# Causal half-width scores with exchanged key halves, and a different split of the output writes, in a decayed linear attention followed by a soft mixture of experts

## The chip, the core and the metric

One core of one Trainium2 chip (8 cores on two dies) runs the program in one launch. The metric is device microseconds of one execution. Times of the kernel before are the median of 3 runs; the profile is of one further execution.

## What is computed

Four batches, 8 heads, 768 positions, 64 channels. Attention without softmax decays by a factor lam per head and position and is computed in blocks with a carried state; its output, as 3072 rows of 512, goes through a soft mixture of 8 experts with 4 slots each.

```python
intra = einsum('bhic,bhjc->bhij', qb, kb) * Dmask      # Dmask[i, j] = lam**(i-j) if i >= j else 0
intra = einsum('bhij,bhjd->bhid', intra, vb)
inter = einsum('bhid,bhde->bhie', qb * lam_pow, kv_state)
out[block] = intra + inter
kv_state = lam**block * kv_state + einsum('bhsd,bhse->bhde', kb * rev_pow, vb)
...
logits = x @ phi                                       # x: 3072 x 512, phi: 512 x 32 slots
slot_input = softmax(logits, axis=0).T @ x
h = maximum(slot_input[e] @ w1[e], 0); slot_out[e] = h @ w2[e]      # 8 experts, 512 -> 1024 -> 512
return softmax(logits, axis=1) @ slot_out
```

Inputs come to 55.1 MB (16.8 MB for w1 and as much for w2 among them), the output to 6.29 MB, all in fp32.

## The kernel before, in words

**Order.** Every engine runs its instructions in the order in which the code issues them (class InOrder). All large loads and all output writes are issued by SyncE (SP) into one hardware queue; SP waits there for a free buffer, or for an earlier DMA.

**Attention (loop over t, lines 485 to 560).** 24 chunks of 128 positions, 6 per batch. For chunk t the loop issues loads for chunk t+2 (q and k turned to channels on the partitions, v, and k once more in natural layout for some chunks; 256 KB each, 12 buffers "ld") and, by the numbers PACE and AHEAD, about three 1 MB tiles of w1 per four chunks (17 buffers "slab"). Then:
- `scores(t)` (lines 223 to 238): for 4 head pairs hp, 2 key halves j and 2 heads hh one matmul with 64 keys as columns of the array and 128 queries moving. The head picks the upper or lower 64 rows of the array, the key half the left or right 64 columns, so four matmuls work in four quarters of the array at a time. Each fp32 matmul shows as two MATMULs.
- `masks(t)`: VectorE multiplies the scores by the decay mask, which is zero for keys behind the query, into `at`.
- `recall(t)`: queries times carried state. `turn_k`: k turned on TensorE for chunks whose natural k is not loaded. `natural(t-1)`: the last output turned to rows.
- `attend(t)` (lines 301 to 318): v times `at`, added to the recalled part; ScalarE copies the result `xt` out of PSUM.
- `state(t)`: decayed keys times v (16 MATMULs of 64 columns), VectorE adds, GpSimd decays. `decay_q`, `decay_k` on GpSimd prepare queries and keys of the next chunk. `kpow`, the decay of keys, is a view of the mask's last column.
- every fourth chunk `logits`, `weights`, `slots`: a running softmax over rows and the slots' inputs.

**Experts (from line 566).** After the last chunk 24 tiles of w2 of 256 KB ("w2t") go into freed buffers of the attention, and ten of 1 MB ("w2p") into slabs, one of them already in chunk 22. `first(0)`, `first(1)` multiply by w1 for four experts each; `shares` (line 700), in the middle of `first(0)`, turns the row softmax into `parts`, a rounded part and its remainder. `CR` (line 711) is an exact copy of the first 256 rows' share. `stack` (line 724) spreads the parts over partitions, in 16 casts of 32 partitions each per 1024 rows. `second(part, ...)` (line 676) multiplies by w2: 16 quads (four expert quarters at a time), part 0 for output columns 0 to 255 and part 1 for 256 to 511; quads 0 to 7 of a part use the first four experts, 8 to 15 the others, and each four need the next two 1 MB tiles.

**Outputs.** `take` copies a finished half of the slots' outputs out of PSUM (ScalarE one half, then VectorE the other); `spread` repeats it over partitions and splits it in two parts; `put(t, half)` makes 256 output rows times 256 columns with two matmuls, copies them on ScalarE or VectorE in turn, and issues the write. `fill` places such puts between the quads of part 1: PUTS says before which quad, 0 standing for a `spread`, n for n puts. Rows below 2*SPLIT*128 are written as two halves of 256 KB, the rest as whole rows of 512 KB.

```python
PUTS = ((2, (0, 1)), (6, (2,)), (8, (2,)), (10, (2,)))
SPLIT = 7
```

Of the kernel before, what the change touches and what calls it, by code (L numbers as in the profile page):

```python
# [14 lines left out]
P = 128  # L15
# [5 lines left out]
SL = 32  # L21
# [9 lines left out]

PUTS = ((2, (0, 1)), (6, (2,)), (8, (2,)), (10, (2,)))
SPLIT = 7
PACE = 76
# [3 lines left out]
def loaded(t):  # L38

    return t % NB in (2, 3) or t % (2 * NB) == 4  # L40


# [16 lines left out]
def decay_attn_soft_moe(  # L59
# [28 lines left out]
    phi_sb = const.tile([P, HP, SL], F32, name="phi_sb")  # L88
    phi_in = const.tile([P, HP, SL], F32, name="phi_in")

# [25 lines left out]
    def load_one(pool_, tag, bufs):  # L116
# [43 lines left out]
    def place_phi():  # L160
        for a in range(2):
            for hh in range(2):
                pool.tensor_copy(
                    out=phi_sb[64 * a:64 * a + 64, 2 * hh:2 * hh + 2],
                    in_=phi_in[64 * hh:64 * hh + 64].rearrange("c (g a) s -> c a g s", a=2)[:, a],
                )
# [15 lines left out]
    own4 = const.tile([P, 4], F32, name="own4")  # L182

    mask = work.tile([P, 2, HP, P], F32, tag="mask", name="mask")
    for hh in range(2):
        for hp in range(HP):
            x = hh * HP + hp
            dve.tensor_tensor_scan(
                out=mask[:, hh, hp, :],
                data0=lam_sb[:, x:x + 1].broadcast_to([P, P]),  # L190
                data1=ident,
                initial=0.0,
                op0=ALU.mult,
                op1=ALU.add,
            )
# [13 lines left out]
    lamc = qpow[:, :, P - 1:P]  # L209
    kpow = mask.rearrange("p a b i -> p (a b) i")[:, :, P - 1:P]  # L210
    CN = const.tile([P, T, SL], F32, name="CN")
    acc = const.tile([P, D], F32, name="acc")
    lsum = const.tile([P, 1], F32, name="lsum")
    e = const.tile([P, P], F32, name="e")
    d = const.tile([P, P], F32, name="d")
    L = const.tile([P, P], F32, name="L")

# [5 lines left out]
    def scores(t):  # L223
        q_, k_ = IN[t, 0], IN[t, 1]
        banks = [bank(x) for x in (("gl", "dp") if t == 0 else ("sc0", "sc1"))]

        for hp in range(HP):
            for j in range(2):
                for hh in range(2):
                    r = slice(64 * hh, 64 * hh + 64)  # L230
                    pe.matmul(
                        out=banks[hh][64 * j:64 * j + 64, hp * P:(hp + 1) * P],
                        lhsT=k_[r, hp * P + 64 * j:hp * P + 64 * j + 64],
                        rhs=q_[r, hp * P:(hp + 1) * P],
                        start=True,
                        stop=True,
                    )
        SC[t] = banks
# [45 lines left out]
    def recall(t):  # L284
        XB[t] = [bank("xa"), bank("xb")]
        if t % NB > 0:

            qs, st = QS.pop(t), ST["st"]
            for hp in range(HP):
                for hh in range(2):  # L290
# [8 lines left out]
                    )  # L299

    def attend(t):
        n = t % NB
        v_ = IN[t, 2].rearrange("p (h c) -> p h c", h=H)
        at = AT.pop(t)
        xt = keep.tile([P, HP, P], F32, tag="xt", name="xt")
        for hh in range(2):
            for hp in range(HP):
                pe.matmul(
                    out=place(t, hh, hp),
                    lhsT=v_[:, HP * hh + hp, :],  # L310
                    rhs=at[hh][:, hp, :],
                    start=(n == 0 and hp < 2),
                    stop=True,
                    skip_group_check=True,
                )
            copy = dve.tensor_copy if t == T - 1 and hh else act.copy
            copy(out=xt[:, 2 * hh:2 * hh + 2], in_=XB[t][hh][:, 0:2 * P].rearrange("p (a b) -> p a b", a=2))
        XT[t] = xt

    def state(t):  # L320
# [134 lines left out]

    blk = const.tile([P, 4, SL], F32, name="blk")
# [3 lines left out]
    const.tile([P, 8], F32, name="fill")  # L460
    sent = 0
    ld1 = (loads, "ld", NLOAD)
    sm = iter(())
    for t in range(T):
# [8 lines left out]
        if t == 0:  # L473
            sp.dma_start(out=phi_in, in_=phi)

# [111 lines left out]
    slots(G - 1)  # L587
    tr = bank("tr")
    for hp in range(HP):
        pe.transpose(tr[:, hp * P:(hp + 1) * P], XT[T - 1][:, hp, :], ident)  # L590
# [3 lines left out]
    act.copy(out=xl[:, 0:HD], in_=tr[:, 0:HD])  # L594
    dl = bank("dp")
    pe.transpose(dl[:, 0:P], el, ident)
    dn = small.tile([P, SL], F32, tag="dn", name="dn", bufs=1)
    dve.tensor_copy(out=dn, in_=dl[:, 0:SL])
    dve.tensor_copy(out=xl[:, HD:D], in_=tr[:, HD:D])

# [96 lines left out]
    load_one(keep, "x", 5)  # L697
    parts, CR = [], []

    def shares():  # L700
# [9 lines left out]
        act.copy(out=parts[0].bitcast(F32R), in_=parts[1])  # L710
        CR.append(half_slab("CR")[:, 0:2 * P].rearrange("p (t c) -> p t c", t=2))
        for n in range(16):
            b, c = divmod(n, 4)
            r = slice(SL * b, SL * b + SL)
            copy = (act.copy, pool.tensor_copy, dve.tensor_copy)[n % 3]
            copy(out=CR[0][SL * c:SL * c + SL, :, r], in_=parts[1][r, 0:2, :])

# [17 lines left out]

    stack((act.copy, pool.tensor_copy, dve.tensor_copy))
    stack((act.copy, pool.tensor_copy, dve.tensor_copy))
    first(1)
    stack((pool.tensor_copy,))
# [21 lines left out]
    def take(half, bank_):  # L761

        x = so[:, half * HD:(half + 1) * HD]
        act.copy(out=x[:, 0:P], in_=bank_[:, 0:P])
        dve.tensor_copy(out=x[:, P:HD], in_=bank_[:, P:HD])

    ow = {}

    def put(t, half):
# [4 lines left out]
        for i in range(2):  # L774
            c_ = CT[t // 8][:, t % 8:t % 8 + 2] if t else CR[0]
            pe.matmul(
                out=pf[:, i * HD:(i + 1) * HD],
                lhsT=c_.rearrange("k t p -> k (t p)").rearrange("k (p i) -> k i p", i=2)[:, i],
                rhs=s4[half] if t else so[:, half * HD:(half + 1) * HD],
                start=True,  # L780
# [12 lines left out]

    pairs = [(t, 0) for t in range(0, 2 * SPLIT, 2)] + [(0, 1)]
    pairs += [(t, 0) for t in range(2 * SPLIT, T, 2)]
    pairs += [(t, 1) for t in (*range(2 * SPLIT, T, 2), *range(2, 2 * SPLIT, 2))]
    pairs.reverse()
# [77 lines left out]
```

## Time and profile before

| | |
|---|---|
| median of 3 runs (lowest to highest) | 167.37 us (166.79 to 169.35) |
| the profiled execution's own time | 167.14 us |
| span of its program on the core | 165.3 us |
| mean granted TensorE clock | 0.976 |
| busy share PE, VectorE, GpSimd, ScalarE | 90%, 55%, 43%, 35% |
| the 16 DMA engines' share on SP's queue | 96.6% |

The profile is read by stage, since shares are means over stages with different limits: attention to about 109 us, w1 to 128 us, w2 to 147.5 us, then outputs alone. PE is TensorE's matmuls, PEld its weight loads, DVE VectorE, ACT ScalarE, POOL GpSimd, SP SyncE. A DMA's landing is its issue in SP's timeline plus the time to landing that the view of DMA issues gives.

### The profile page before, as it was taken

The page shows a single profiled execution, that of the slowest core. Times are in us where ns is not written, and L with a number is a line of the kernel's source. Part 1 is how long each engine was busy: PE and PEld are TensorE (multiplying, and loading weights), DVE is VectorE, ACT ScalarE, POOL GpSimd, SP SyncE. Part 2 cuts the span into 40 slices and gives each one's busy share as a digit, 9 for nine tenths or more (in the row PEclk, how much of TensorE's full clock was granted, in tenths as well). Part 3 has the DMA queues.
Part 4 walks back from the last instruction along what each step waited for, and adds up shares of the span by engine and source line. Part 5 has one row for each costly group of instructions (what it writes and reads, how often), then busy time and mean ns, then how long its engine had stood idle before and what let it go on. Part 6 is the DMA issues. An engine that isn't in the chain of part 4 may idle for free.

```text
span 165.3 us, 6275 instructions
## 1 busy us (share of the span) xinstructions
PE 149.1 (90%) x2651; PEld 109.0 (66%) x2651; DVE 90.3 (55%) x208; ACT 58.5 (35%) x147; POOL 71.8 (43%) x108
## 2 busy tenths in 40 slices
PE   6999999999989999999999999998999989989400
PEld 6778878677868878788868896863323455648300
DVE  2964445447744574568655775564388821328600
ACT  3134412443443444231635152242055902226400
POOL 2786790277447227766119665300022894000000
PEclk9999999999999999999999999999999999999955
DMA  5999999999999999999999999999999999982897
GB/s 165 357 418 392 312 363 414 410 423 401 412 416 402 417 409 408 410 350 344 402 415 401 415 391 394 404 390 367 375 336 396 418 416 423 396 302 76 362 402 251
DMA packets 25131, 61.82 MB, mean 374 GB/s; under 512 B 2576, under 2 KB 6288, under 8 KB 23056
## 3 DMA queue, kind: packets, MB, share of 16 engines
q1 hardware_dynamic: 24960, 61.42, 96.6%
q8 instruction: 21, 0.34, 0.7%
q14 instruction: 6, 0.05, 0.1%
q10 hardware_dynamic: 144, 0.01, 0.1%
HBM read 55.12 MB, written 6.29 MB: 371 GB/s over the span
## 4 chain that ended last, share of the span: by engine, by line
PE 66%; DVE 9%; DMA 5%; ACT 5%; POOL 4%; issue 3%; DVEq 0%; POOLq 0%; ACTq 0%
PE xa L53 17%; PE sc L53 14%; PE kv L53 10%; PE xb L53 8%; PE gl L53 8%; PE tr L53 7%; DMA w2t<-w_x 3%; DVE o L53 3%; ACT ct L53 2%; DVE mask L53 2%; DMA lam_sb<-lam_x 2%; POOL kd L53 2%; PE dp L53 2%; POOL qs L53 1%; DVE hz L53 1%
## 5 line engine op out<-in xcount | busy, mean ns | idle before, releaser
L53 DVE TENSOR_TENSOR at<-sc,mask 128x512 f32<-128x512 f32 x46 | 29.6, 685 | 15.4 <-PE sc L53 14.6
L53 ACT COPY x<-tr 128x512 f32<-128x512 f32 (+1 forms) x24 | 13.9, 578 | 37.7 <-PE tr L53 37.7
L53 POOL TENSOR_TENSOR qs<-ld,qpow 128x512 f32<-128x512 f32 x20 | 25.5, 1275 | 2.1 <-POOL kd L53 2.1
L53 PE MATMUL sc<-ld 64*64 64x128 f32 x736 | 26.0, 276 | 0.1
L53 PEld LDWEIGHTS sc<-ld 64*64 64x64 f32 x736 | 20.3, 133 | 6.2 <-issue 3.4
L53 POOL TENSOR_TENSOR dec<-st,qpow 128x256 f32<-128x256 f32 x16 | 9.9, 621 | 25.6 <-DVE st L53 25.5
L53 POOL TENSOR_TENSOR kd<-kn,mask 128x512 f32<-128x512 f32 x10 | 10.6, 1058 | 12.8 <-ACT kn L53 12.4
L53 PE MATMUL xa<-at,ld 128*64 128x128 f32 x192 | 15.8, 284 | 0.0
L53 DVE TENSOR_TENSOR st<-dec,kv 128x256 f32<-128x256 f32 x16 | 6.7, 422 | 16.5 <-PE kv L53 15.1
L53 PE MATMUL tr<-ident,xt 128*128 128x128 f32 x96 | 15.4, 283 | 0.0
L53 PE MATMUL xb<-at,ld 128*64 128x128 f32 x192 | 14.6, 273 | 0.1
L53 PE MATMUL xa<-qs,st 64*64 64x128 f32 x160 | 14.0, 274 | 0.7 <-POOL qs L53 0.3
L53 PE MATMUL xb<-qs,st 64*64 64x128 f32 x160 | 13.1, 274 | 0.6 <-issue 0.6
L53 PE MATMUL kv<-ld,kd 128*64 128x64 f32 x320 | 12.9, 223 | 0.1
L53 PEld LDWEIGHTS tr<-ident,xt 128*128 128x128 f32 x96 | 10.4, 141 | 3.8 <-issue 3.8
L53 POOL CAST ct<-part 32x256 fp32r<-32x256 f32 x26 | 10.3, 395 | 5.0 <-DVE part L53 3.9
L53 PEld LDWEIGHTS xa<-at,ld 128*64 128x64 f32 x192 | 10.0, 136 | 3.7 <-issue 1.6
L53 PEld LDWEIGHTS kv<-ld,kd 128*64 128x64 f32 x320 | 11.9, 138 | 0.8 <-issue 0.5
L53 PEld LDWEIGHTS xa<-qs,st 64*64 64x64 f32 x160 | 9.9, 133 | 3.0 <-issue 1.9
L53 PEld LDWEIGHTS xb<-at,ld 128*64 128x64 f32 x192 | 11.0, 137 | 0.3 <-issue 0.2
L53 POOL TENSOR_TENSOR kd<-ld,mask 128x512 f32<-128x512 f32 x10 | 10.6, 1059 | 0.0
L53 PEld LDWEIGHTS xb<-qs,st 64*64 64x64 f32 x160 | 9.4, 133 | 0.2 <-ACT xt L53 0.2
(148 smaller groups left out, 233.8 us busy)
## 6 DMA issues: line engine op xcount, KB each, us to landing
slab<-w_x SPq DMA_DIRECT2D x16, 1024.0 KB, 8.4
w2p<-w_x SPq DMA_DIRECT2D x10, 1024.0 KB, 10.6
ld<-qT SPq DMA_DIRECT2D x24, 256.0 KB, 6.8
ld<-kT SPq DMA_DIRECT2D x24, 256.0 KB, 6.5
ld<-vN SPq DMA_DIRECT2D x24, 256.0 KB, 7.5
w2t<-w_x SPq DMA_DIRECT2D x24, 256.0 KB, 5.4
y<-o SPq DMA_DIRECT2D x14, 256.0 KB, 4.0
ld<-kN SPq DMA_DIRECT2D x10, 256.0 KB, 7.2
```

What stands on the lines that cost most here:

```text
L53: return self._tc.keep_in_program_order(f(*args, **kwargs))
```

## The change

**Scores.** From chunk 2 on, matmuls of the second key half take only the 64 queries that can see them. For head pairs 2 and 3 (`plain` is false) the two key halves change places in the array and in PSUM; their mask is built from an identity with exchanged halves (`d`), `vs` holds v of these heads with exchanged halves, copied by ScalarE in two copies of 64 partitions after each `attend`, and `kpow` becomes a tile of its own, put together by three VectorE copies. Score banks are the same two tiles from chunk 1 on.

**Experts and outputs.** `CR` goes; all outputs use the parts. The second of the three `stack` calls moves behind `first(1)`. The last four units of w2 come as two DMAs of 1 MB by row half i instead of by expert pair. `take` is one ScalarE copy. Part 1 has one spread before quad 8 and nine first-half puts before quad 12, with no puts elsewhere; behind it one first half, then second halves, with the last three row groups as whole rows.

```diff
-PUTS = ((2, (0, 1)), (6, (2,)), (8, (2,)), (10, (2,)))
-SPLIT = 7
+PUTS = ((8, (0,)), (12, (9,)))
+SPLIT = 9
...
+def plain(hp):
+    return hp < HP // 2
...
+    def load_four():
+        Q, x, _ = units[-1]
+        units.clear()
+        for i in range(2):
+            t_ = slabs.tile([P, 4, 512], F32, tag="slab", name="w2p")
+            src = w2[4 * Q:4 * Q + 4, x:x + 2].rearrange("e x p d -> e (x p d)")
+            sp.dma_start(out=t_, in_=src.rearrange("e (p i d) -> i p e d", p=P, i=2)[i])
...
+    for j in range(2):
+        dve.tensor_copy(out=d[:, 64 * j:64 * j + 64], in_=ident[:, 64 - 64 * j:128 - 64 * j])
...
-                data1=ident,
+                data1=ident if plain(hp) else d,
...
-    kpow = mask.rearrange("p a b i -> p (a b) i")[:, :, P - 1:P]
+    kpow = const.tile([P, H, 1], F32, name="kpow")
+    k2 = kpow.rearrange("p (a b) o -> p a b o", a=2)
+    dve.tensor_copy(out=k2[:, :, 0:2], in_=mask[:, :, 0:2, P - 1:P])
+    for j in range(2):
+        dve.tensor_copy(
+            out=k2[64 * j:64 * j + 64, :, 2:4], in_=mask[64 - 64 * j:128 - 64 * j, :, 2:4, P - 1:P]
+        )
...
-        for hp in range(HP):
-            for j in range(2):
+        for hp in (0, 2, 1, 3):
+            for col in (1, 0):
+                j = col if plain(hp) else 1 - col
+                x = hp * P + (64 if j and t > 1 else 0)
...
-                        out=banks[hh][64 * j:64 * j + 64, hp * P:(hp + 1) * P],
+                        out=banks[hh][64 * col:64 * col + 64, x:(hp + 1) * P],
...
-                        rhs=q_[r, hp * P:(hp + 1) * P],
+                        rhs=q_[r, x:(hp + 1) * P],
...
+    def turn_v(t):
+        if t < T:
+            v_ = IN[t, 2].rearrange("p (b h c) -> p b h c", b=2, c=DH)
+            for j in range(2):
+                act.copy(out=vs[64 * j:64 * j + 64], in_=v_[64 - 64 * j:128 - 64 * j, :, 2:4])
...
-                    lhsT=v_[:, HP * hh + hp, :],
+                    lhsT=v_[:, HP * hh + hp, :] if plain(hp) else vs[:, hh, hp - 2, :],
...
         XT[t] = xt
+        turn_v(t + 1)
...
     stack((act.copy, pool.tensor_copy, dve.tensor_copy))
+    first(1)
     stack((act.copy, pool.tensor_copy, dve.tensor_copy))
-    first(1)
     stack((pool.tensor_copy,))
...
-        act.copy(out=x[:, 0:P], in_=bank_[:, 0:P])
-        dve.tensor_copy(out=x[:, P:HD], in_=bank_[:, P:HD])
+        act.copy(out=x, in_=bank_[:, 0:HD])
...
-            c_ = CT[t // 8][:, t % 8:t % 8 + 2] if t else CR[0]
+            c_ = CT[t // 8][:, t % 8:t % 8 + 2]
...
-    pairs = [(t, 0) for t in range(0, 2 * SPLIT, 2)] + [(0, 1)]
-    pairs += [(t, 0) for t in range(2 * SPLIT, T, 2)]
-    pairs += [(t, 1) for t in (*range(2 * SPLIT, T, 2), *range(2, 2 * SPLIT, 2))]
+    pairs = [(t, 0) for t in range(0, 2 * SPLIT + 2, 2)]
+    ends = [(t, half) for t in range(2 * SPLIT, T, 2) for half in range(2)][1:]
+    for t in range(0, 2 * SPLIT, 2):
+        pairs += [(t, 1), *ends[:1]]
+        del ends[:1]
```

Also: phi comes in through the tile `L`, the last chunk's turned output uses two PSUM banks behind the turned weights instead of one ahead of them, and some tiles go.

**What stands in a row now.** On PE, around the first scores of the loop (chunk 2; `sc` are the two score banks, `xa` and `xb` the outputs of `attend`, `kv` the state), before:

```order
L53 MATMUL xa<-at,ld 64x128 x4
L53 MATMUL xb<-at,ld 64x128 x4
L53 MATMUL kv<-ld,kd 64x64 x8
L53 MATMUL sc_306<-ld 64x128
L53 MATMUL sc_307<-ld 64x128
```

and now:

```order
L58 MATMUL xa<-at,ld 64x128 x2
L58 MATMUL xa<-at,vs 64x128 x2
L58 MATMUL xb<-at,ld 64x128 x2
L58 MATMUL xb<-at,vs 64x128 x2
L58 MATMUL kv<-ld,kd 64x64 x8
L58 MATMUL sc_177<-ld 64x64
L58 MATMUL sc_178<-ld 64x64
L58 MATMUL sc_177<-ld 64x128
L58 MATMUL sc_178<-ld 64x128
L58 MATMUL sc_177<-ld 64x128
L58 MATMUL sc_178<-ld 64x128
L58 MATMUL sc_177<-ld 64x64
```

Sixteen score matmuls of 128 columns have become eight of 64 and eight of 128, and half of `attend` reads `vs`.

On PE, part 1 of w2 with its puts (`xa` the quads, four rows' matmuls each; `gl` the spread; `<-ct` the puts), before:

```order
L53 MATMUL xa<-w2p,hz 32x256 x8
L53 MATMUL gl<-so,blk 128x256
L53 MATMUL tr<-so,CR 128x256 x2
L53 MATMUL xa<-w2p,hz 32x256 x16
L53 MATMUL sc_2548<-ct 128x256 x2
L53 MATMUL sc_2554<-ct 128x256 x2
L53 MATMUL xa<-w2p,hz 32x256 x8
L53 MATMUL dp<-ct 128x256 x2
L53 MATMUL kv<-ct 128x256 x2
L53 MATMUL xa<-w2p,hz 32x256 x8
L53 MATMUL tr<-ct 128x256 x2
L53 MATMUL sc_2592<-ct 128x256 x2
```

and now:

```order
L58 MATMUL xa<-w2p,hz 32x256 x32
L58 MATMUL gl<-so,blk 128x256
L58 MATMUL xa<-w2p,h 32x256 x16
L58 MATMUL tr<-ct 128x256 x2
L58 MATMUL sc_2565<-ct 128x256 x2
L58 MATMUL sc_2570<-ct 128x256 x2
L58 MATMUL dp<-ct 128x256 x2
L58 MATMUL kv<-ct 128x256 x2
L58 MATMUL tr<-ct 128x256 x2
L58 MATMUL sc_2592<-ct 128x256 x2
L58 MATMUL sc_2598<-ct 128x256 x2
L58 MATMUL dp<-ct 128x256 x2
```

Seven puts in four places have become nine in one row, ahead of the last four quads.

On DVE, between the two halves of the experts (`ct` the casts of `stack`, `hz` and `h` the hidden layer that part 0 waits for), before:

```order
L53 STREAM_TRANSPOSE hz<-CR 128x512 x2
L53 TENSOR_TENSOR part<-part 128x768
L53 COPY ct<-part 32x8x32 x10
L53 TENSOR_SCALAR hz<-tr,rown 128x512
L53 STREAM_TRANSPOSE hz<-hz 128x512 x2
```

and now:

```order
L58 STREAM_TRANSPOSE hz<-h 128x512 x2
L58 TENSOR_TENSOR part<-part 128x768
L58 COPY ct<-part 32x8x32 x5
L58 TENSOR_SCALAR h<-tr,rown 128x512
L58 STREAM_TRANSPOSE h<-h 128x512 x2
L58 COPY ct<-part 32x8x32 x5
```

Five of ten casts have moved behind the hidden layer's work.

## Rows read from the trace of the kernel before

**Rows 1.** The page's span in 40 equal slices: share of the DMA engines in tenths.
```profile
DMA  5999999999999999999999999999999999982897
```

**Rows 2.** The page's bytes.
```profile
HBM read 55.12 MB, written 6.29 MB: 371 GB/s over the span
```

**Rows 3.** Windows of 5 us: PE, PEld, DVE, ACT, POOL busy, PEclk, DMA share, GB/s.
```profile
40.00:45.00 5.00, 4.96 (x126) 4.36 (x127) 3.83 (x9) 1.76 (x6) 2.73 (x4) 1.00 1.04 413
70.00:75.00 5.00, 5.00 (x132) 4.52 (x132) 3.31 (x7) 1.84 (x5) 2.96 (x4) 1.00 1.00 351
75.00:80.00 5.00, 5.00 (x142) 4.39 (x136) 3.73 (x9) 1.76 (x6) 2.80 (x3) 1.00 1.01 358
120.00:125.00 5.00, 5.00 (x52) 1.53 (x48) 3.72 (x10) 3.16 (x9) 1.15 (x5) 1.00 0.94 335
```

**Rows 4.** SP's timeline, four single issues: start, us to issue, what.
```profile
125.60 0.41 SPq L53 DMA_DIRECT2D w2p<-w_x  x1
...
128.16 0.43 SPq L53 DMA_DIRECT2D w2p<-w_x  x1
...
150.13 0.53 SPq L53 DMA_DIRECT2D y<-o  x1
...
161.30 0.59 SPq L53 DMA_DIRECT2D y<-o  x1
```

**Rows 5.** DMA issues around each of those four: KB, us to landing.
```profile
w2p<-w_x SPq DMA_DIRECT2D x1, 1024.0 KB, 14.2
...
w2p<-w_x SPq DMA_DIRECT2D x1, 1024.0 KB, 17.2
...
y<-o SPq DMA_DIRECT2D x1, 256.0 KB, 2.4
...
y<-o SPq DMA_DIRECT2D x1, 256.0 KB, 3.1
```

**Rows 6.** DMA rate in 40 slices of 144:156, then of 153:162.5.
```profile
GB/s 393 372 348 372 393 263 150 382 379 369 420 355 362 297 82 85 72 51 48 0 0 0 0 0 174 382 314 3 0 0 0 137 410 423 437 410 396 410 423 437
...
GB/s 0 0 379 414 431 397 431 397 431 414 431 397 431 397 448 397 448 379 449 414 448 414 431 414 414 448 397 431 289 371 392 380 388 384 380 397 371 388 384 384
```

**Rows 7.** The chain that ended last, in chunks 10 and 11: start, us, what.
```profile
52.70 0.44 PE xb L53 x8
53.14 0.46 PE kv L53 x16
53.60 1.03 PE sc L53 x32
```

**Rows 8.** Groups in attention: one ScalarE copy, one small VectorE operation; busy, mean ns.
```profile
L53 ACT COPY xt<-xa 128x256 f32<-128x256 f32 x17 | 6.3, 368 | 1.2 <-PE xa L53 1.1
...
L53 DVE TENSOR_SCALAR gm<-gsel,nm 128x4 f32<-128x4 f32 x1 | 0.2, 231 | 0.0
```

**Rows 9.** SP's waits in 115:119: us in total, times, longest.
```profile
SPq L53 <- PE kv L53: 2.0, 1, 2.0
```

**Rows 10.** Timeline from 126 us: start, us, engine, operation, count.
```profile
126.81 4.20 DVE L53 CAST ct<-part 32x256 fp32r<-32x256 f32 x10
...
137.32 0.70 PE L53 MATMUL gl<-so,blk 128*128 128x256 f32 x2
...
144.73 2.80 PE L53 MATMUL xa<-w2p,hz 128*32 128x256 f32 x48
...
150.25 0.43 DVE L53 TENSOR_TENSOR ct<-xb,ct 64x256 fp32r<-64x256 f32 x1
...
151.46 0.51 PE L53 MATMUL kv<-ct 128*128 128x256 f32 x2
...
154.20 0.41 PE L53 MATMUL dp<-ct 128*128 128x256 f32 x2
```

**Rows 11.** Windows of 1 us at PE's end; columns as in rows 3.
```profile
154.00:155.00 1.00, 0.60 (x5) 0.40 (x4) 1.00 (x3) 0.98 (x2) 0.00 (x0) 1.00 1.05 426
...
157.00:158.00 1.00, 0.00 (x0) 0.00 (x0) 0.00 (x0) 0.00 (x0) 0.00 (x0) 0.71 1.02 418
```

More of the change, by code (lines that the diff above doesn't have):

```diff
@@ L88, in decay_attn_soft_moe @@
     phi_sb = const.tile([P, HP, SL], F32, name="phi_sb")
-    phi_in = const.tile([P, HP, SL], F32, name="phi_in")
+    vs = const.tile([P, 2, 2, DH], F32, name="vs")
+    L = const.tile([P, P], F32, name="L")
+    d = const.tile([P, P], F32, name="d")
     IN = {}
@@ L121, in load_one @@
         wt["w2", Q, q, x, i] = t_
+    def load_four():
[5 more added lines that the diff above has]
+            sp.dma_start(out=t_, in_=src.rearrange("e (p i d) -> i p e d", p=P, i=2)[i])
+            for q in range(4):
+                wt["w2", Q, q, x, i] = t_[:, q]
     def load_two():
+        if len(units) == 4:
+            return load_four()
         (Q, x, q), other = units.pop(), units.pop()
@@ L164, in place_phi @@
                     out=phi_sb[64 * a:64 * a + 64, 2 * hh:2 * hh + 2],
-                    in_=phi_in[64 * hh:64 * hh + 64].rearrange("c (g a) s -> c a g s", a=2)[:, a],
+                    in_=L[64 * hh:64 * hh + 64].rearrange("c (g a s) -> c a g s", a=2, s=SL)[:, a],
                 )
@@ L214, in decay_attn_soft_moe @@
     e = const.tile([P, P], F32, name="e")
-    d = const.tile([P, P], F32, name="d")
-    L = const.tile([P, P], F32, name="L")
     AT, XT, X, ST, QS, KD = {}, {}, {}, {}, {}, {}
@@ L224, in scores @@
         q_, k_ = IN[t, 0], IN[t, 1]
-        banks = [bank(x) for x in (("gl", "dp") if t == 0 else ("sc0", "sc1"))]
-        for hp in range(HP):
-            for j in range(2):
+        if t < 2:
+            SC["banks"] = [bank(x) for x in (("gl", "dp") if t == 0 else ("sc0", "sc1"))]
+        banks = SC["banks"]
+        for hp in (0, 2, 1, 3):
+            for col in (1, 0):
+                j = col if plain(hp) else 1 - col
+                x = hp * P + (64 if j and t > 1 else 0)
                 for hh in range(2):
@@ L453, in slots @@
             )
-    blk = const.tile([P, 4, SL], F32, name="blk")
+    blk = small.tile([P, 4, SL], F32, tag="blk", name="blk", bufs=1)
     blk_ = blk.rearrange("p g s -> p (g s)")
@@ L459, in decay_attn_soft_moe @@
     gm = const.tile([P, 4], F32, name="gm")
-    const.tile([P, 8], F32, name="fill")
     sent = 0
@@ L473, in decay_attn_soft_moe @@
         if t == 0:
-            sp.dma_start(out=phi_in, in_=phi)
+            sp.dma_start(out=L, in_=phi.rearrange("p a s -> p (a s)"))
         for _ in range((2, 4, 3)[t - T + 3] if t >= T - 3 else 0):
@@ L488, in decay_attn_soft_moe @@
             scores(1)
+            turn_v(0)
         elif t > 1:
@@ L587, in decay_attn_soft_moe @@
     slots(G - 1)
-    tr = bank("tr")
+    dl = bank("dp")
+    pe.transpose(dl[:, 0:P], el, ident)
+    tr = [bank(x) for x in ("tr", "sc1")]
     for hp in range(HP):
-        pe.transpose(tr[:, hp * P:(hp + 1) * P], XT[T - 1][:, hp, :], ident)
+        pe.transpose(tr[hp // 2][:, hp % 2 * P:(hp % 2 + 1) * P], XT[T - 1][:, hp, :], ident)
     xl = keep.tile([P, D], F32, tag="x", name="x", bufs=5)
@@ L593, in decay_attn_soft_moe @@
     act.activation(out=selw, in_=sel, func=AF.Copy, scale=wgt)
-    act.copy(out=xl[:, 0:HD], in_=tr[:, 0:HD])
-    dl = bank("dp")
-    pe.transpose(dl[:, 0:P], el, ident)
+    act.copy(out=xl[:, 0:HD], in_=tr[0][:, 0:HD])
     dn = small.tile([P, SL], F32, tag="dn", name="dn", bufs=1)
     dve.tensor_copy(out=dn, in_=dl[:, 0:SL])
-    dve.tensor_copy(out=xl[:, HD:D], in_=tr[:, HD:D])
+    dve.tensor_copy(out=xl[:, HD:D], in_=tr[1][:, 0:HD])
     si = bank("xa")
@@ L697, in decay_attn_soft_moe @@
     load_one(keep, "x", 5)
-    parts, CR = [], []
+    parts = []
     def shares():
@@ L710, in shares @@
         act.copy(out=parts[0].bitcast(F32R), in_=parts[1])
[L711 to L716, printed above, removed]
     first(0, shares)
@@ L778, in put @@
                 lhsT=c_.rearrange("k t p -> k (t p)").rearrange("k (p i) -> k i p", i=2)[:, i],
-                rhs=s4[half] if t else so[:, half * HD:(half + 1) * HD],
+                rhs=s4[half],
                 start=True,
```

## The prediction

> **What bounds the kernel now.** I read the page's slices first, then the byte counts, the windows, SP's issues with their landings, the chain, and last the timeline of the tail. The slices show the DMA engines at nine tenths or more from the second slice to the 36th, a dip, and full work again to the end [rows 1]. 61.4 MB have to move [rows 2], and a good window moves 413 GB/s [rows 3], which makes 149 us for the bytes alone out of a span of 165.3. So the transfers are the first bound, and the question for each edit is whether it lets them run more tightly.
>
> They lose time in two kinds of places. In the stream of loads, windows such as 70:75 and 75:80 (351 and 358 GB/s) and 120:125 (335) fall behind 413 although PE is busy throughout [rows 3]. At the end of the loads comes a hole. The last load of w2 is issued at 128.16 and lands 17.2 us later, at 145.4; the last write lands at 161.30 + 3.1 = 164.4 [rows 4, 5]. In between are 19.0 us. A piece of 256 KB as half rows moves at about 385 GB/s, 0.68 us; the same bytes as whole rows at about 415 GB/s, 0.63 us [rows 6], by the last eleven slices and by those ahead of them. The kernel before has 14 half-row pieces and 10 pieces' worth of whole rows: 14 x 0.68 + 10 x 0.63 = 15.8 us. The other 3.2 us are the hole, seen as slices of 0 to 85 GB/s after 148 us [rows 6]: seven first halves stand ready behind the loads, and the next write is issued only at 150.13, after the last quads (144.73 + 2.80 = 147.5 [rows 10]), and lands 2.4 us later [rows 5].
>
> In attention the chain runs through PE nearly without a break, one chunk being scores, recall, transposes, attend and state [rows 7]. PE sets there when buffers come free, and so when SP can issue.
>
> **Scores.** 32 MATMULs take 1.03 us [rows 7], eight in each quarter of the array. The prices of one step: `xb`, 8 MATMULs of 128 columns, two at a time, 0.44 / 4 = 0.11 us; `kv`, 16 of 64 columns, two at a time, 0.46 / 8 = 0.058 us. A quarter now has four of each instead of eight long ones, since the exchanged heads put a short one where the others have a long one: 4 x (0.11 - 0.058) = 0.21 us less per chunk, 4.6 us over 22 chunks. The bounds are 0 (if a short one kept its quarter as long as a long one) and 4.6; I take 3.5, as the first chunks wait for GpSimd as well, and the start loses a little.
>
> **What scores cost.** At the start three VectorE copies for `kpow` come ahead of the first decayed keys, and two for `d` ahead of the masks. The nearest row is a 128x4 operation of 0.23 us [rows 8]: 0 if all lie beside the load of lam, 5 x 0.23 = 1.2 if none; I take 0.5, the two for `d` being hidden and the three not. The copies of v are two of 64x256 per chunk, at most 0.37 us each [rows 8]. On ScalarE, 35% busy, they stand behind the copies of `xt`; queued behind them is the next chunk's copy of rows, which PE needs one chunk later. So they cost 0; if ScalarE's slack were gone, or v landed late (it is now wanted almost a chunk earlier), up to 0.74 per chunk, 16 us in all. The row nearest to the case is ScalarE's idle wait for PE, so 0.
>
> **What PE's lead does to the loads.** It can't shorten transfers, only the low windows. 120:125 is low because SP stood 2.0 us waiting for PE, for a slab that the first half of `first(0)` frees [rows 9]; with PE 3.5 us ahead this wait goes, and of 5 x (1 - 335/413) = 0.9 us I count 0.8. The two windows from 70 us lose 10 x (1 - 354/413) = 1.4 us; I count half, 0.7. The later start takes 0.4 back. The loads end 1.1 to 1.2 us earlier, near 144.2; bounds 0 and, with all low windows made good and nothing lost, 3 us.
>
> **The hidden layer.** Ten casts held VectorE for 4.20 us [rows 10] ahead of the second hidden layer; five stand there now, so part 0 ends some 1 to 2 us earlier. This goes into PE's lead and not into the sum: part 1 then waits for its tiles. The waits that end last in part 1 are loads: quads 8 to 11 need the tile that lands at 125.60 + 14.2 = 139.8, 5.6 us ahead of the last one [rows 4, 5].
>
> **The tail.** Call the landing of the last load L. Quads 8 to 11 start at L - 5.6 and take 4 x 0.47 (48 MATMULs, six quads, 2.80 us [rows 10]), 1.9. Nine puts follow at (154.20 - 151.46) / 9 = 0.30 to 0.33 us each [rows 10], 3.0 us. Quads 12 to 15 then end at L - 5.6 + 1.9 + 3.0 + 1.9 = L + 1.2; the split of the last tiles by row half lets 12 and 13 start on the first one. Before, from the end of the quads to the first new write were 150.13 - 147.53 = 2.6 us, with an exact first put and no spread ahead of it. The spread adds 0.70 on PE, about 0.37 on ScalarE and 0.43 on VectorE [rows 8, 10], 1.5 us; `take` in one copy and the cheaper matmul give back up to 0.8. So the first second-half write is issued 3.3 to 4.1 us after the quads and lands 2.4 later, at L + 6.9 to L + 7.7. The nine first halves are done at L + 9 x 0.68 = L + 6.1, the tenth would be due at L + 6.8: a hole of 0.1 to 0.9, I take 0.4. Later puts come every 0.3 us and never starve 0.68. The writes now are 18 half-row and 6 whole-row pieces: 18 x 0.68 + 6 x 0.63 = 16.0, which costs 0.2.
>
> The Trainium skill, "DMA: Bandwidth & Descriptors", section "Bandwidth", asks for DMAs of 1 MiB and more to reach three quarters of the peak, which speaks against more writes of 256 KB. By its table such a write would run at perhaps half the peak (an estimate between its sizes), near 1.2 us, and four more of them would cost about 2 us. The trace doesn't agree: pieces that stand in a queue follow each other at 385 GB/s [rows 6], and only the lone one shows 2.4 us [rows 5].
>
> **The sum.** 19.0 becomes 16.0 + 0.4 = 16.4: 2.6 less. The loads end 1.2 earlier. The profiled execution took 167.14 us, 1.8 more than its span, and 167.14 - 3.8 = 163.3. Its time is 0.2 below the median of the three runs, so against the median this is 2.4%, little more than the 2% which a measurement of this kernel can tell from no change (164.0).
>
> **Rivals.**
> - *PE's lead ends at the loads.* The DMA engines were full nearly all the time [rows 1], and the low windows have their cause in the transfers (70:80 has a share of 1.00, so something was always under way). Then only the tail gains: 167.14 - 2.6 = 164.5, within 2%. Against it: SP's wait for PE [rows 9] and the 0.94 in 120:125.
> - *All low windows close.* PE's lead keeps buffers free everywhere, the loads end 3 us earlier and the hole goes entirely: 167.14 - 3.2 + 0.2 - 3.0 = 161.1. For it: PE sets nearly every release. Against it: windows that are low at a full share.
> - *The array slows in front of quad 8.* With PE ahead, quads 4 to 7 end and PE waits for the tile at L - 5.6, some 2.3 us if quads 4 to 7 waited for theirs as well. After PE's last matmul (within 154:155) the granted clock was 1.00 and in 157:158 it was 0.71 on average [rows 11], so it left the higher level (2.4 GHz) for 1.2 GHz between two and four us into the idle time. If it falls here and stays, eight quads cost 8 x 0.47 = 3.7 us more, and nine puts, at 0.8 for their two matmuls, 4.5 more: 163.3 + 8.2 = 171.5, slower than before. It is slower than before from 4 us of delay on, that is if the clock stays low through the puts; if it comes back after quads 8 to 11, 165.2. Against it: the wait is shorter than the idle time that the row shows ahead of the fall. The Trainium skill, "TensorE: Matmul & The Clock Gate", section "Why this matters for your kernels", warns of idle gaps of PE between bursts of matmuls in the same sense.
> - *The short matmuls bring nothing*, a quarter staying taken as long as before: PE is then 0.5 us later at the start and 1 to 2 earlier from the hidden layer on, and the time is the first rival's, up to 165.
>
> **How the numbers follow.** Forecast (163.3) 0.44; lead ends at the loads, or short matmuls bring nothing (164.5 to 165) 0.30; all low windows close (161.1) 0.15; slow array with an early recovery (165.2) 0.06, with a late one (171.5) 0.05. The forecast's case lies under 164.0 with nine parts in ten, the first rival's with one in ten: faster by over 2% 0.40 + 0.03 + 0.15 = 0.58; slower by over 2% 0.05; the rest, 0.37, within 2%. The range 161.0 to 165.8 leaves out the late recovery and some of the ends.
>
> **What would show it.** Right: scores' groups of 32 MATMULs near 0.82 us in the chain; attention's last `attend` 3 to 4 us earlier than 109; SP without the 2.0 us wait; the last load near 144; no slice of 0 GB/s between the last load and the end; nine writes landing at 0.68 us. Wrong: a load end near 145.4 in spite of an earlier attention, idle slices behind the ninth write, a PEclk below 1.00 ahead of quad 8, ScalarE or PE waiting for `vs` or for v in attention, or scores still at 1.03.

## The result and the profile after

The changed kernel takes **165.5 us** (median of 10 runs, 164.41 to 167.29); the kernel before, measured beside it on the same chip, 167.47 us. The ratio is 0.985 (95% interval 0.982 to 0.988): 1.5% faster, less than the 2% that the prediction called measurable, inside its range of 161.0 to 165.8, and 2.2 us above the predicted 163.3. The profiled execution took 164.78 us with a span of 163.0.

First the scores, the part that the forecast's working rests on. One group in the page: out<-in, shapes, count, then busy us and mean ns, idle before. Before:

```profile
L53 PE MATMUL sc<-ld 64*64 64x128 f32 x736 | 26.0, 276 | 0.1
```

After, with the copies of v that the change adds on ScalarE:

```profile
L58 PE MATMUL sc<-ld 64*64 64x128 f32 (+1 forms) x736 | 21.4, 252 | 0.6 <-issue 0.3
...
L58 ACT COPY vs<-ld 64x256 f32<-64x256 f32 x48 | 19.3, 403 | 1.2
```

The busy time falls by 26.0 - 21.4 = 4.6 us, which is the sum of the prediction to the tenth. Little of it became a lead. The last `attend` of the kernel before ended at 109.22; here it is the row at 108.38, and ends at 108.77 (PE's timeline: start, us, engine, operation, count):

```profile
108.38 0.39 PE L58 MATMUL xb<-at,vs 128*64 128x128 f32 x4
```

That is 0.45 us earlier, where 3.5 were forecast. This is what PE waited for in attention (10 to 110 us; us in total, times, longest), in the kernel before:

```profile
PE xb L53 <- issue: 0.6, 1, 0.6
PE xa L53 <- POOL qs L53: 0.3, 1, 0.3
PE xa L53 <- issue: 0.3, 1, 0.3
PE dp L53 <- DMA w2t<-w_x: 0.2, 1, 0.2
```

and in the changed one:

```profile
PE xa L58 <- issue: 1.4, 2, 1.0
PE xa L58 <- POOL qs L58: 1.1, 4, 0.6
PE gl L58 <- issue: 1.0, 1, 1.0
PE sc L58 <- issue: 0.3, 1, 0.3
```

1.4 us of waits became 3.8. So 2.4 of the 4.6 us went straight into waiting, and some 0.5 into a later start (chunk 1's attend ends at 13.78 instead of 13.30). Waits for GpSimd's `qs` make 0.8 us of the growth; the larger part, 1.8 us, are stretches marked "issue", for which this view names no cause. The two longest, in chunks 9 and 16, both stop PE in the middle of a group of matmuls:

```profile
45.11 0.32 PE L58 MATMUL xa<-qs,st 64*64 64x128 f32 x1 [1.03 <-issue]
...
76.31 1.08 PE L58 MATMUL gl<-xt,phi_sb 128*32 128x128 f32 x31 [1.03 <-issue]
```

The last section says what these stretches go together with. The lead grew to 1.5 us by chunk 14 (its attend ends at 68.67 instead of 70.16) and was gone at chunk 16 (78.41, and 78.18 before), and from there transfers stand in the chain. This is the chain of 66 to 90 us by line; in the kernel before, the chain of 60 to 112 us holds no transfer but one of w2t (11.1%):

```profile
by line: DMA ld<-qT 31.0%; DMA ld<-kN 27.1%; PE xa L58 11.9%; PE tr L58 7.3%; PE sc L58 7.2%; POOL qs L58 5.2%; PE xb L58 4.4%; POOL dec L58 2.6%; issue 2.0%; PE kv L58 1.9%; SPq L58 0.1%; POOLq L58 0.1%
```

The windows that answer to [rows 3] (PE, PEld, DVE, ACT, POOL busy, PEclk, DMA share, GB/s), and one of 95 to 105 us:

```profile
70.00:75.00 5.00, 5.00 (x126) 4.26 (x125) 3.56 (x8) 2.14 (x5) 3.86 (x5) 1.00 1.05 399
75.00:80.00 5.00, 3.97 (x113) 3.53 (x112) 1.94 (x8) 2.51 (x8) 1.63 (x2) 1.00 1.04 417
95.00:105.00 10.00, 10.00 (x238) 8.20 (x234) 5.90 (x13) 6.67 (x19) 5.89 (x7) 1.00 1.01 382
120.00:125.00 5.00, 5.00 (x52) 1.49 (x48) 4.15 (x7) 1.87 (x4) 0.03 (x1) 1.00 1.00 389
```

The loads did gain where the forecast looked: 351 and 358 GB/s became 399 and 417, and 335 became 389. In 95 to 105 they gave a little back (394 before). PE, full in 75 to 80 before, now idles a fifth of it, which is the second of the two stretches above. The wait of SP for PE that [rows 9] showed, 2.0 us, did not go; it is 2.5:

```profile
SPq L58 <- PE kv L58: 2.5, 1, 2.5
```

The last load is issued at 127.78 and lands 15.7 us later, at 143.5 (128.16 and 17.2 in [rows 4, 5]):

```profile
w2p<-w_x SPq DMA_DIRECT2D x1, 1024.0 KB, 15.7
```

The tail, in windows of 1 us with the same columns:

```profile
142.00:143.00 1.00, 1.00 (x10) 0.97 (x8) 1.00 (x3) 1.00 (x3) 0.00 (x0) 1.00 0.34 131
143.00:144.00 1.00, 1.00 (x12) 0.61 (x15) 1.00 (x2) 0.90 (x3) 0.00 (x0) 1.00 0.65 233
144.00:145.00 1.00, 1.00 (x24) 0.64 (x20) 0.19 (x1) 0.25 (x1) 0.00 (x0) 1.00 1.19 394
145.00:146.00 1.00, 0.95 (x15) 0.34 (x5) 0.03 (x1) 0.37 (x1) 0.00 (x0) 1.00 1.02 362
146.00:147.00 1.00, 0.68 (x2) 0.28 (x2) 0.66 (x1) 0.28 (x1) 0.00 (x0) 1.00 0.18 54
147.00:148.00 1.00, 0.40 (x3) 0.40 (x4) 0.43 (x1) 0.09 (x1) 0.00 (x0) 1.00 0.41 144
148.00:149.00 1.00, 1.00 (x10) 1.00 (x10) 0.60 (x1) 0.84 (x2) 0.00 (x0) 1.00 1.08 381
```

There are two holes, and neither stands where the forecast had put one, behind the ninth write. In the first, at 142 to 143.5, most DMA engines are through with the loads and the first write has only just been issued, at 142.08. In the second, at 146 to 147.6, SP issues nothing: its fifth write takes 2.13 us to issue, where its neighbours take 0.6 (SP's timeline):

```profile
144.83 2.13 SPq L58 DMA_DIRECT2D y<-o  x1
```

The last write lands at 161.92, 18.4 us behind the last load: 19.0 before, 16.4 forecast. Behind the second hole the writes follow each other at 0.66 to 0.71 us per half and 1.25 per 512 KB, without a gap. One execution does not fix this number: the profiles of e1, e3, e5 and e9 below, with the same order of puts and writes, show 17.3 to 17.5 us.

### The profile page after: what moved, and what is told of

Its sections match the earlier page's. It is cut to its first block, busy times and chain, and to the rows that moved or that the text cites. A ratio compares the mean times of both kernels' runs of the same rounds, so it can differ in the third digit from the quotient of the medians.

```text
span 163.0 us, 6311 instructions
## 1 busy us (share of the span) xinstructions
PE 144.1 (88%) x2647; PEld 105.2 (65%) x2647; DVE 87.1 (53%) x206; ACT 76.3 (47%) x189; POOL 70.8 (43%) x103
## 4 chain that ended last, share of the span: by engine, by line
PE 63%; DMA 14%; POOL 8%; DVE 5%; issue 2%; ACT 0%; DVEq 0%; POOLq 0%; SPq 0%
PE xa L58 18%; PE kv L58 10%; PE tr L58 9%; PE gl L58 8%; PE sc L58 8%; PE xb L58 8%; DMA ld<-qT 5%; DMA ld<-kN 4%; POOL qs L58 4%; DMA w2t<-w_x 3%; DVE o L58 2%; DMA lam_sb<-lam_x 2%; POOL kd L58 2%; DVE mask L58 2%; PE dp L58 2%
## 5 line engine op out<-in xcount | busy, mean ns | idle before, releaser
L58 PEld LDWEIGHTS sc<-ld 64*64 64x64 f32 x736 | 17.9, 133 | 6.8 <-issue 2.2
L58 PE MATMUL sc<-ld 64*64 64x128 f32 (+1 forms) x736 | 21.4, 252 | 0.6 <-issue 0.3
L58 ACT COPY vs<-ld 64x256 f32<-64x256 f32 x48 | 19.3, 403 | 1.2
L58 POOL TENSOR_TENSOR kd<-kn,kpow 128x512 f32<-128x512 f32 x10 | 10.4, 1042 | 14.7 <-ACT kn L58 14.1
L58 PEld LDWEIGHTS xa<-qs,st 64*64 64x64 f32 x160 | 9.2, 132 | 3.4 <-issue 1.8
L58 POOL TENSOR_TENSOR kd<-ld,kpow 128x512 f32<-128x512 f32 x10 | 10.4, 1042 | 0.0
L58 PE MATMUL xa<-at,ld 128*64 128x128 f32 x96 | 10.4, 295 | 0.0
L58 PE MATMUL xa<-at,vs 128*64 128x128 f32 x96 | 9.6, 274 | 0.4 <-issue 0.4
L58 ACT COPY xt<-xa 128x256 f32<-128x256 f32 x24 | 8.9, 369 | 1.8 <-PE xa L58 1.7
L58 PE MATMUL xb<-at,ld 128*64 128x128 f32 x96 | 9.5, 273 | 0.0
```

The costliest lines, as they stand in the source:

```text
L58: return self._tc.keep_in_program_order(f(*args, **kwargs))
```

## The experiments

Three theories were at stake. **Tail:** the gain lies in the outputs alone. **Lead:** PE's shorter scores pull the loads forward. **Other bounds:** PE's lead is eaten by GpSimd and by transfers. All ratios are to the kernel before on the same chip.

**One half at a time.** e1 is the kernel before with the new order of experts and outputs; e2 has the new attention and the old experts and outputs; e3 is the changed kernel without the exchange of halves.

e1, on the kernel before (its core):

```diff
-PUTS = ((2, (0, 1)), (6, (2,)), (8, (2,)), (10, (2,)))
-SPLIT = 7
+PUTS = ((8, (0,)), (12, (9,)))
+SPLIT = 9
...
+        if len(units) == 4:
+            return load_four()
...
-            c_ = CT[t // 8][:, t % 8:t % 8 + 2] if t else CR[0]
+            c_ = CT[t // 8][:, t % 8:t % 8 + 2]
```

> The attention of the kernel before with the experts and outputs of the changed one. Theory A (PE's lead in attention is lost to loads that arrive no earlier; the gain is the tail's): the tail alone brings nearly the whole of the 1.5%, 165.3 to 166.0 us. Theory B (the scores let the loads end 1.8 us earlier, and the tail brings the 0.6 us by which the time from the last load to the end fell from 19.0 to 18.4 us): 166.5 to 167.0 us. In the trace A wants the last load within 0.7 us of the 143.5 of the changed kernel, B wants it near 145.3.

Measured: 165.68 us, 0.989 (0.982 to 0.996).

e2, on the changed kernel, is the same edit backwards:

```diff
-PUTS = ((8, (0,)), (12, (9,)))
-SPLIT = 9
+PUTS = ((2, (0, 1)), (6, (2,)), (8, (2,)), (10, (2,)))
+SPLIT = 7
...
```

> The attention of the changed kernel with the experts and outputs of the one before. Theory A: attention ends within 0.6 us of before and the time is 166.8 to 167.6 us. Theory B: the last load lands near 143.5 us and the time is 165.2 to 166.0 us. Both expect score groups of about 0.90 us in place of 1.10.

Measured: 167.25 us, 0.997 (0.994 to 1.001).

e3, on the changed kernel:

```diff
 def plain(hp):
-    return hp < HP // 2
+    return True
...
-        turn_v(t + 1)
```

> The changed kernel without the exchange of key halves: the second key half still takes 64 queries, but all heads keep their place, so one half of the array has only long matmuls and ScalarE copies no v. Theory A (loads bound attention): the time stays within 0.4 us of the changed kernel's. Theory B (PE's lead counts): scores go back to about 1.05 us a chunk and 0.9 to 1.8 us are lost. A third way, that the 48 copies of v on ScalarE cost something, makes it faster than the changed kernel by up to 1 us.

Measured: 165.56 us, 0.988 (0.983 to 0.993).

So the outputs alone bring all that can be told from the whole change, and 4.6 us less work on PE bring at most 0.6%. The intervals of e1, e3 and the whole change overlap, so no effect of the exchange of halves can be told here. e3 leaves out the copies of v together with the exchange's gain and can't split the two. The times are the first theory's; the signs in the traces are mixed. e1's last load lands at 145.43, where the second theory wanted it, and its last write 17.4 us later. In e2 attention ends at 108.56 and the last load lands at 144.13, 1.2 us earlier than in the kernel before, and yet the time hardly moves: its last write comes 19.6 us later.

**Spreading the puts.** e4 gives the writes an earlier start: the spread ahead of quad 4, three puts ahead of quad 8, six ahead of quad 12. e8 goes further; e7 is e4's spread on the attention of the kernel before.

```diff
-PUTS = ((8, (0,)), (12, (9,)))
+PUTS = ((4, (0,)), (8, (3,)), (12, (6,)))
```

and in e8

```diff
-PUTS = ((8, (0,)), (12, (9,)))
+PUTS = ((2, (0,)), (4, (2,)), (8, (4,)), (12, (3,)))
```

> The changed kernel with the first spread before quad 4 instead of 8, three puts before quad 8 and six before quad 12. Theory A (the DMA engines run dry from 142.3 to 143.4 us since the first write is issued only at 142.1, when most engines have finished their loads): that hole closes, the first write is issued about 3 us ahead of the last load, and the time falls by 0.7 to 1.2 us against the changed kernel. Rival (that hole is made up for later, or the quads end later by what the puts take): no change within 0.4 us.

Measured: 164.0 us, 0.980 (0.975 to 0.985).

> The changed kernel with the first spread before quad 2, two puts before quad 4, four before quad 8 and three before quad 12. If what is lost around the last load is writes that are issued too late, this is at least as fast as e4_early_puts, 163.3 to 164.2 us. If early puts hold back the quads that wait for loads, it is slower than e4_early_puts by 0.5 us or more.

Measured: 164.27 us, 0.980 (0.975 to 0.986).

> The attention of the kernel before, with the experts and outputs of the changed one and the puts of e4_early_puts (first spread before quad 4, three puts before quad 8, six before quad 12). Theory A (the scores bring next to nothing, the order of the tail brings the gain): within 0.7 us of e4_early_puts, 164.0 to 164.8 us. Theory B (the scores bring 1 us and more): 165.0 us and over.

Measured: 164.7 us, 0.983 (0.976 to 0.989).

The medians of e4 and e8 lie 1.2 to 1.5 us below the changed kernel's, but the intervals overlap with its 0.982 to 0.988; the clean comparison is e9 with e10 further down. e7 stands 0.7 us above e4, at the edge of its first theory, and e8 a little outside the range that it was given. In e4 the rate in 142 to 146, where the changed kernel had its first hole, is 341 to 402 GB/s:

```profile
142.00:143.00 1.00, 1.00 (x17) 0.44 (x8) 0.00 (x0) 0.00 (x0) 0.00 (x0) 1.00 1.04 402
143.00:144.00 1.00, 1.00 (x9) 1.00 (x10) 0.61 (x2) 0.38 (x1) 0.00 (x0) 1.00 1.06 393
144.00:145.00 1.00, 1.00 (x13) 0.69 (x15) 1.00 (x3) 0.98 (x3) 0.00 (x0) 1.00 1.00 360
145.00:146.00 1.00, 0.70 (x16) 0.14 (x5) 0.27 (x1) 0.33 (x1) 0.00 (x0) 1.00 0.96 341
```

Its last write lands 16.0 us behind its last load (145.97 to 162.02), in e7 16.5. So nine puts in one row seem to come too late to stand behind the loads, as the trace of the changed kernel had suggested. Starting still earlier, in e8, brings nothing more.

**Are the loads crowded by w1?** e5 issues the tiles of w1 about a chunk later.

```diff
-AHEAD = 40
+AHEAD = -40
```

> The changed kernel with AHEAD at -40 instead of 40: each 1 MB tile of w1 is issued about one chunk later, so that the chunks' own loads stand ahead of it; the bytes are the same. If PE's lead in attention is lost to loads of q and k that arrive too late (theory A), attention ends 1.5 to 3 us earlier than the changed kernel's 108.8 us, and the total, set by the bytes, stays within 0.8 us of it. If the lead is lost inside PE's own work or to GpSimd (rival), attention ends within 0.7 us of 108.8.

Measured: 166.14 us, 0.992 (0.988 to 0.996): 0.6 us above the changed kernel. Holding back w1 gives nothing. Its profile, of a longer execution (167.84 us), ends attention at 110.72, which neither reading had expected.

**Does PE's time still count?** e6 leaves out the score matmuls of head pairs 1 and 3 from chunk 2 on, so its output lacks their part.

```diff
-        for hp in (0, 2, 1, 3):
+        for hp in (0, 2, 1, 3) if t < 2 else (0, 2):
```

> The changed kernel, leaving out the score matmuls of head pairs 1 and 3 from chunk 2 on, so that about another 0.4 us per chunk, 9 us in all, goes from PE. Theory A (loads bound the attention): the time stays within 1 us of the changed kernel's 165.5 us. Theory B (PE's time counts): at least 3 us faster.

Measured: 161.36 us, 0.962 (0.956 to 0.968). Four microseconds below the changed kernel. That attention is bound by its transfers alone falls with it. It is not a clean measure of PE's busy time, though: its last `attend` ends at 103.05, but from 15 to 25 us its loads already ran at 418 GB/s where the changed kernel's ran at 362. Without these matmuls the loads wait there for the release of other buffers, and the wait of SP for GpSimd that the changed kernel shows at that place is gone. e6 also issues fewer instructions on PE (2295 matmuls for 2647), and none of its idle stretches of PE in attention is one without a named cause. In the changed kernel (the window from 15 to 25 us, then SP's waits in 13:18):

```profile
15.00:25.00 10.00, 9.38 (x230) 7.89 (x226) 4.83 (x9) 4.91 (x12) 9.24 (x14) 1.00 1.02 362
...
SPq L58 <- PE kv L58: 2.9, 1, 2.9
SPq L58 <- POOL kd L58: 1.8, 1, 1.8
```

In the second wait a load stands until GpSimd has read the keys in `decay_k`, and GpSimd comes to that only after `dec`, the decayed state, for which it waits itself (its timeline in the changed kernel):

```profile
14.86 0.62 POOL L58 TENSOR_TENSOR dec<-st,qpow 128x256 f32<-128x256 f32 x1 [1.26 <-DVE st L58]
15.44 1.04 POOL L58 TENSOR_TENSOR kd<-ld,kpow 128x512 f32<-128x512 f32 x1
```

The state needs PE's `kv`, done at 14.25, so a faster PE starts this chain earlier; but the 2.2 us from there to the end of `kd`, at 16.48, are VectorE's and GpSimd's. The kernel before has the same wait of 1.8 us, and 351 GB/s in that window. This gave the last theory: the early hole is GpSimd's, and PE's lead has nothing to act on until it is gone.

**GpSimd's order.** e9 is the changed kernel with `kd` ahead of `dec`. e10 has that and e4's puts. e11 has both on the attention of the kernel before, e12 both without the exchange of halves.

```diff
         ST["st"] = st
+        if n > 0:
+            decay_k(t + 1)
         if n < NB - 2:
             dec = work.tile([P, HP, DH], F32, tag="dec", name="dec")
...
             state(t)
-        decay_k(t + 1)
+        if opens or t % NB == NB - 1:
+            decay_k(t + 1)
```

> The changed kernel, with one swap on GpSimd: the decayed keys of the next chunk (kd) are computed ahead of the decayed state (dec) instead of behind it. In the trace of the changed kernel the loads fall to 362 GB/s in 15:25 while SyncE waits 1.8 us for a kd, as in the kernel before, and no lead of PE helps there. Theory A (the early hole is GpSimd's, and what it costs stays to the end): SyncE's wait for kd under 1.0 us, 15:25 near 390 GB/s, the loads end about 0.8 us earlier and the time is about 164.7, ratio to the kernel before 0.980. Theory B (the loads would only meet PE sooner later on and give it back in 95:115): the window is better but the time stays at 165.5, ratio 0.985. If dec, now about 0.5 us later, holds up the state: the time above 166.

Measured: 164.8 us, 0.985 (0.979 to 0.990). The wait and the window moved as expected:

```profile
SPq L58 <- POOL kd L58: 0.7, 1, 0.7
...
15.00:25.00 10.00, 9.84 (x238) 8.35 (x234) 5.16 (x10) 4.95 (x12) 9.12 (x14) 1.00 1.05 413
```

but by itself the swap cannot be told from the changed kernel. The loads, some 0.4 MB ahead at 25 us, gave about half of it back in 95 to 115 (374 GB/s against 383), as the second theory of the expectation had it, and most of the rest ahead of that; and the late puts stayed.

> The same swap on GpSimd with the puts spread as in the run e4 (one ahead of quad 4, three ahead of quad 8, six ahead of quad 12). If the two gains lie in different places they add up: about 163.2, ratio 0.974. If the early hole costs nothing: as e4, ratio 0.980.

Measured: **163.13 us, 0.973 (0.969 to 0.977)**, the best of all versions that do the whole work, and faster than both kernels. Beside e9, on the same chip, it differs in the puts alone: 1.7 us, and the intervals (0.979 to 0.990 and 0.969 to 0.977) lie apart. So the earlier puts are shown to count.

> The attention of the kernel before (full-width scores, no exchange) with the same swap on GpSimd and the same spread puts as e10. Theory A (GpSimd's early hole had hidden what the shorter scores give): e10 is then at least 0.8 us below this one, about 164.0 here, ratio 0.980. Theory B (the loads set attention's end whatever PE saves in scores): within 0.5 us of e10.

Measured: 164.52 us, 0.981 (0.977 to 0.985). The six runs of e10 lie between 162.6 and 163.66, those of e11, on the same chip beside them, between 163.91 and 165.21. So with the swap and the earlier puts the new attention is worth 1.4 us. In the profiles its attention ends at 108.23 against 109.22:

```profile
107.84 0.39 PE L58 MATMUL xb<-at,vs 128*64 128x128 f32 x4
...
108.61 0.61 PE L53 MATMUL xb<-at,ld 128*64 128x128 f32 x8
```

That is 1.0 us of 4.6, so most of the saving is still lost here. And that it was the swap which let this much through is not shown: with the same puts and no swap, e4 lies 0.7 us below e7 (0.980 and 0.983, on two chips, overlapping), and neither e4 and e10 nor e7 and e11, which differ in the swap alone, have intervals that lie apart.

> The run e10 (kd ahead of dec, puts spread) without the exchange of halves: the scores are still left out for early queries, but every short matmul stands in one column half, and the copies of v and the split masks are gone. In e3, the same without the swap on GpSimd, score matmuls kept PE busy for 25.8 us, as full-width ones do (26.0), against 21.4 with the exchange. Theory A (PE's 4.6 us count once GpSimd's early hole is gone): busy 25.8 us again and the time that of e11, ratio near 0.981 and at least 0.6% above e10. Theory B (e10 gained from something other than PE's time in scores): ratio within 0.3% of e10, 0.973.

Measured: 165.05 us, 0.982 (0.977 to 0.988), as e11. Its scores:

```profile
L58 PE MATMUL sc<-ld 64*64 64x64 f32 (+1 forms) x736 | 26.0, 251 | 1.5 <-DMA ld<-kT 0.9
```

26.0 us, exactly as much as full-width scores, though half of the matmuls are half as long and the mean of one, 251 ns, is that of the exchanged version (252). The short ones then all stand in one column half of the array, and the other half has eight long ones as before. Shorter matmuls alone save nothing; the 4.6 us come only with the exchange.

## Why the prediction was right and wrong

The time lies in the range, but the sum reached 3.8 us where the median moved by 2.0 and the profiled execution by 2.4, and the range held it partly by luck: the loads ended earlier than forecast, only half for the forecast's reasons, and that made up for part of the tail. Term by term, in the order of the prediction:

- **Scores, 0.21 us per chunk: right.** 4.6 us over the kernel, and e12 shows that the reason was right too: a quarter of the array costs what its own matmuls cost.
- **"I take 3.5" as PE's lead: wrong, 0.45 measured.** This is the step that failed first. The prediction allowed 1.1 us for GpSimd and the start; the start took its 0.5, but waits grew by 2.4 us: 0.8 for `qs` from GpSimd, and 1.8 in stretches for which the profile names no cause (a wait for w2t of 0.2 went); from chunk 16 on the chain runs over loads. Some 1.2 us more are not assigned. The prediction had read that PE is busy without a break as PE being the bound by a wide margin; the lead stopped growing at 1.5 us.
- **Copies of v at no cost: not refuted.** ScalarE does 48 copies, 19.3 us, and went from 35% to 47% busy; e3, without them and without the exchange's gain, is no faster. PE never waits for `vs`, but the copies hold v's buffers, and SP stands for them (over the whole span; what that costs was not tried apart):

```profile
SPq L58 <- ACT vs L58: 3.5, 9, 1.1
```

- **Loads end 1.2 us earlier: right in this execution, for half of the reasons.** It was 1.8 (145.34 to 143.51). The windows from 70 us closed almost wholly instead of half. 120:125 gained 5 x (389 - 335) / 413 = 0.65 for the 0.8 reckoned, but not because SP's wait went: PE was hardly earlier there, and the wait grew, so the low window was not this wait's doing alone. The bound of 3 us was loose: the three low windows of [rows 3] make 2.3, and 15 to 25 us, as low as they (351 GB/s), is not among them. The later start is priced at 0.5 and taken off as 0.4, and of 1.1 to 1.2 the sum takes the upper end. And the term is soft: e4, with the same attention, landed its last load at 145.97 and e2 at 144.13, partly since writes share the queue with the last loads in e4. e2, which has the scores and with them most of this term, moved the time by 0.3%.
- **The hidden layer: right.** Five casts of 2.00 us in place of [rows 10]'s ten of 4.20 stand ahead of the second hidden layer:

```profile
124.84 2.00 DVE L58 CAST ct<-part 32x256 fp32r<-32x256 f32 x5
...
128.20 0.75 DVE L58 TENSOR_SCALAR h<-tr,rown 128x512 f32<-128x512 f32 x1 [1.36 <-PE tr L58]
```

- **The tail, 19.0 to 16.4: the term that was mis-sized most; it measured 18.4, and 17.3 to 17.5 in e1, e3, e5 and e9.** The prices were right (half rows 0.66 to 0.71 us each, no gap behind the ninth write, part of the puts faster than reckoned: nine in 2.7 us). What failed is the line "the nine first halves are done at L + 9 x 0.68": it let the writes start at the landing of the last load, as if they already stood in the queue. PE's timeline shows why they did not:

```profile
138.42 0.70 PE L58 MATMUL gl<-so,blk 128*128 128x256 f32 x2
139.05 1.93 PE L58 MATMUL xa<-w2p,h 128*32 128x256 f32 x32
140.92 0.51 PE L58 MATMUL tr<-ct 128*128 128x256 f32 x2
...
143.56 1.93 PE L58 MATMUL xa<-w2p,h 128*32 128x256 f32 x32
```

  The spread that the change puts ahead of quad 8 is missing from the line of the quads. Their tile landed at 138.42, L - 5.1 in place of L - 5.6, and with the spread in front of them quads 8 to 11 start at 139.05, not at 137.9; the first put is at 140.92, and its write is issued at 142.08, when 1.4 us are left to L. With the spread placed earlier and puts from quad 8 on (e4) the tail is 16.0, even under the forecast's, though there some writes go ahead of the last load. The second hole, 0.86 + 0.63 = 1.5 us by the windows of 146 to 148 against 385 GB/s, goes with one slow issue on SP, which nothing in the trace of before had foretold. Slow issues of 1.1 to 1.9 us stand near this place in e1, e3, e5 and e9 too, so it is no accident of one execution.
- **Quads 12 to 15 end at L + 1.2:** they end at 145.49, L + 2.0, by the later tile and the same spread, less what the nine puts were faster.
- **The clock: right.** PE had no idle stretch ahead of quad 8, and the granted clock stayed at 1.00 (2.4 GHz) until PE had ended (1.00 in 152:153, 0.79 in 153:154); the rival that the array slows did not come about.
- **The Trainium skill's rule** ("DMA: Bandwidth & Descriptors", section "Bandwidth"), which asks for DMAs of 1 MiB and more, would have made each half-row write much dearer. The trace still disagrees for writes that queue: 0.66 to 0.71 us for 256 KB, against 1.25 for 512 KB.

Of the rivals, "PE's lead ends at the loads" (164.5) came nearest, in mechanism too: e2 shows the scores worth 0.3%. It is not the whole of it, though, since e6 and e10 still gain from less work on PE, and PE's stretches without a named cause are no loads.

## What to carry to other kernels

Before pricing a faster engine, ask of each stretch what would end next there: another engine that frees the buffers, a transfer, or the engine's own supply of instructions. Here 4.6 us of saved matmul time moved the time by at most 0.6% by itself, and by 1.4 us once two GpSimd instructions were swapped and the writes came earlier. Writes that are to follow the last loads must be issued before the last load lands, so price the chain of PE, copy and issue up to the first write, not only the transfers. When matmuls share the array by quarters, count the work of the fullest quarter, since the mean duration of one matmul (251 ns without the exchange, 252 with it) doesn't tell.

## What the hardware showed besides

PE's stretches without a named cause go together with packets of instructions. The DMA records hold 16 KB instruction packets of one queue, mostly 5 to 7 us apart in attention. The two stretches of 1.03 us above end at 45.11 and 76.31; the last such packets before them start at 42.79 and 73.97, 2.3 us earlier both times. It is the rule in this case: between 5 and 113 us the fourteen profiles have 41 idle stretches of PE over 0.2 us that are marked "issue", and each of them ends 2.2 to 2.4 us after such a packet starts; the 25 with a named cause that come behind such a packet end anywhere from 0.1 to 6.3 us after it starts. The number of packets follows PE's work: 21 in the changed kernel, with 2647 matmuls and as many weight loads, and 18 in e6, with 2295. So PE most likely stands there waiting for its own instructions. Shorter matmuls would use these up faster; the sums agree but scatter, 0.6 to 2.2 us in the four profiles with the old attention and 1.9 to 3.8 in the seven with the new one. No run changed the number of instructions by itself, so this is argued and not shown.

A slow issue on SP in the tail came together with a long packet of instructions. In 140 to 152 us of the changed kernel the DMA view has one instruction packet of 16 KB, taking 0.9% of 16 engines over 12 us, which is 1.7 us; it starts at 144.84, as the issue of 2.13 us does at 144.83:

```profile
q1 hardware_dynamic: 3226, 3.69, 84.9%
q8 instruction: 1, 0.02, 0.9%
```

Elsewhere in this run such packets take 0.9 to 1.0 us, but for one of 1.32 at 94.82. The same pair stands in e1 (issue 1.89 us, packet 1.40, at 146.7), e3 (1.89 and 1.40, at 148.6), e7 (1.57 and 1.40, at 146.4) and e9 (1.77 and 1.24, at 144.9). In e10 the packet at 146.3 takes 0.96 us and the issue beside it 0.59. Which of the two delays the other was not tried; in e7 the slow issue cost no gap in the landings, as writes issued earlier stood in the queue.

The engines of the DMA queue also do not end together: the rate was down to 131 GB/s in 142 to 143, while the last load landed at 143.5. And the landing of the last load is no clean mark: it moved by up to 2.5 us between profiles with the same attention (143.51 in the changed kernel to 145.97 in e4), where three writes had been issued ahead of it in the one and six in the other, so that a single trace does not settle a term of one microsecond there.
